# First MLP in four token groups of 432, attention values kept unsplit, last score rows on array quadrants

## The chip, the cores and the metric

One core of a Trainium2 chip runs one program. The metric is device time in microseconds (us); less is better. TensorE (PE) multiplies, with its weight loads shown as a stream of its own (PEld); VectorE (DVE), ScalarE (ACT) and GpSimd (POOL) do elementwise work; SyncE (SP) issues all DMAs from one queue, in order.

## The reference

Three stages in float32, 2304 tokens of 512 features:

```
scores = q @ k.T / 8, blocks of 64, block-causal mask   (batch 4, heads 8, seq 576, head_dim 64)
x = softmax(scores) @ v          -> tokens x 512
h = max(x @ w1, x @ w2, x @ w3)  -> 768 features;  y = h @ w_out          (first MLP)
u = max(y @ w_in, 0);  out = (u * u) @ w_out2     -> 2048 features, back to 512   (second MLP)
```

The four batch entries are independent in the attention only; in the MLPs every token is treated alike, so a group of tokens may be cut anywhere, across entries too.

## The kernel before

**Arithmetic.** TensorE has a fast format, float32r, that keeps fewer bits. For full precision most products are made of three float32r products: each operand is split into a high part (a cast) and a low part (the difference), and lo·hi, hi·lo and hi·hi are summed in PSUM. Where an operand is left as plain float32 (F32 tiles), one matmul in the program does the product, and the trace then shows two matmul records for it.

**Attention.** A pair of heads is one unit; 16 pairs, 4 for each entry. A pair has score steps of 128 rows (`step`, i = 0 to 3) and a last step (`last_step`) for its last 64 rows. Steps 0 and 1 belong to token group 0 (256 tokens), the others to group 1 (320 tokens). In the last step the 64 rows of both heads make 128 rows against 576 keys, in two halves of 288 keys (`sc_t0`, `sc_t1`), each in its own PSUM bank. For the four pairs of the first entry (`S_F32`) these scores are plain float32: one matmul for each head with a stationary tile of 128 rows and 64 columns, so two heads fill the two column halves of the array. For the other 12 pairs `score_operands` loads zero-padded queries `zt` and keys `kt`, splits both (`z2h`, `z2l`, `k2h`, `k2l`), and each half is three float32r matmuls of 128x128 by 288. Then come a maximum (DVE), an exponential (ACT), transposes against the identity (`tp`, PE) and the product with v (`av`, PE, column halves again).

**First MLP.** `mlp1(b, g)` handles one group: 18 accumulators of 12 matmuls (L1), then 4 accumulators of 18 (L2): 288 matmuls, each as wide as the group, 256 or 320 columns. There are 8 groups. Its input parts sit in `xhl0` and `xhl1`, one buffer for each group size, its hidden parts in `hh` and `hl`, one buffer each. The first entry's values are split as they leave PSUM; the other entries' values wait as float32 in `xf` and `split_x` splits them. The results `y` go to DRAM.

**Weight forms and second MLP.** All weights are converted on DVE, ACT and POOL. The second MLP's weights are turned into seven linear forms for each of 8 slices q (`up_forms`, `quad_forms`), split, and stored to DRAM; the second MLP (three passes of `up` and `down`, all matmuls 384 columns wide) streams them back through a ring of 9 tiles `ws`.

**Order.** All operations are recorded first, and a planner (`Plan.issue`) orders them by dependencies, ranks and the durations that `duration` gives. Attention has rank 0 and the first MLP rank 1, so MLP matmuls fill the gaps of attention. Every engine then runs its list strictly in order. The line of every operation in the profile is the planner's own, so the profile is read by tile names.

Of the kernel before, what the change touches and what calls it, by code (L numbers as in the profile page):

```python
# [12 lines left out]
F32 = mybir.dt.float32  # L13
# [11 lines left out]
NPAIR = H // 2  # L25
# [15 lines left out]
GA, GB = 256, 320  # L41
SCALE = 0.125
PAIRS = B * NPAIR

CFG = dict(PD=-1, PE=1, A1=0, A2=0, WP=1, FC=(8, 16), WO=24, FI=0, LO2=0, HI2=0, Q2=0, RN=3, XL=2, HL=2, SO=0, TF=0, W_A=0.7, W_B=1.5, SPARE='hl..rhl..rhl..r..r..r', S=15, PB=3, QB=(2, 2, 3), BANKS=(3, 2, 1, 2), LO=0, HI=0, Q=0, EV=('*', '*'), EV2=('a', 'a'), CB=2, PC=0, PM=1000, PX=-0.5, PO=0, HH='*', XH='*', N0='a', YS='a', HIS=0, RB=1, TB=(2, 1), KB=1, CT='a', LT='d', XA=4, XB=0)
# [302 lines left out]
def fused_kernel(ctx: ExitStack, tc: tile.TileContext, z0, k0, qk, v, w123, wo1, win2, wo2, out):  # L348
# [31 lines left out]
    def load_w_(src, hi, lo, name, f=None, raw=None):  # L380
        spare = SPARE[len(chunks)] if len(chunks) < len(SPARE) else "."
        chunks.append(name)
        if raw is not None:
            pass
        elif spare in "hl":
            both = m1.tile([128, 512, 3], U32, tag="h" + spare, name=f"raw_{name}").rearrange("p n t -> p (n t)")
            raw, f = both[:, :1024].rearrange("p (n t) -> p n t", t=2), both[:, 1024:].bitcast(F32)
        elif spare == "r":
            raw = at.tile([128, 512, 2], U32, tag="raw", bufs=CFG["RB"], name=f"raw_{name}")
            f = m1.tile([128, 512], F32, tag="xf", bufs=4, name=f"f_{name}")  # L390
# [68 lines left out]
    def score_operands(n):  # L459
# [27 lines left out]
        z2 = [z.rearrange("p h q -> p (h q)") for z in z2]  # L487
        return score, [(z2[1], k2[0]), (z2[0], k2[1]), (z2[0], k2[0])]
# [26 lines left out]
    def new_x(b, g):  # L515
        if (b, g) not in x_t:
            w = GROUPS[g][1]
            both = m1.tile([128, 2, KC, w], F32R, tag=f"xhl{g}", name=f"xhl{b}_{g}")
            x_t[b, g] = [both[:, i] for i in range(2)]
        return x_t[b, g]  # L520
# [8 lines left out]
    def attn_pair(n, groups=(0, 1)):  # L529
# [13 lines left out]
        if n not in xf_t and not direct:  # L543
            xf_t[n] = m1.tile([128, S], F32, tag="xf", bufs=4, name=f"xf{n}")
        xf = xf_t.get(n)
# [60 lines left out]
        def last_step():  # L606
# [31 lines left out]
        def values(g):  # L638
# [10 lines left out]
            if direct:  # L649
                rs = at.tile([128, GB], F32, tag="rs", name=f"rs{n}_{g}")  # L650
                nc.scalar.copy(out=rs[:, :w], in_=sum_rows(g)[:, :w])
                xh, xl = [t[:, n % NPAIR] for t in new_x(n // NPAIR, g)]
# [30 lines left out]
    def split_x(b, g):  # L683
        with nc.ranked(CFG["PX"]):
            split_x_(b, g)

    def split_x_(b, g):
        a, w = GROUPS[g]
        for hp in range(NPAIR):
            n = b * NPAIR + hp  # L690
            xf = xf_t[n][:, a:a + w]
            xh, xl = [t[:, hp] for t in new_x(b, g)]
            cp(CFG["XH"], out=xh, in_=xf)
            (nc.vector if CFG["XL"] == 2 or CFG["XL"] and b + 1 == B else nc.gpsimd).tensor_tensor(out=xl, in0=xf, in1=xh.bitcast(F32), op=ALU.subtract)
# [7 lines left out]
    def mlp1(b, g):  # L702
        with nc.ranked(1):
            mlp1_(b, g)

    def mlp1_(b, g):
        xh, xl = x_t[b, g]
        a, w = GROUPS[g]
        hh = m1.tile([128, NC1, GB], F32R, tag="hh", name=f"hh{b}_{g}")
        hl = m1.tile([128, NC1, GB], F32R, tag="hl", name=f"hl{b}_{g}")  # L710
# [7 lines left out]
        for c in range(NC1):  # L718
            run = None
            hi, lo = w1[c]  # L720
            for i in range(3):
                acc = acc_bank(f"l1_{b}_{g}_{c}_{i}")
# [4 lines left out]
                nxt = m1.tile([128, GB], F32, tag="run", bufs=CFG["RN"], name=f"run{b}_{g}_{c}_{i}")  # L727
# [6 lines left out]
            with urgent():  # L734
                cp(CFG["HH"], out=hh[:, c, :w], in_=run[:, :w])
                (nc.vector if CFG["HL"] == 2 or CFG["HL"] and b + 1 == B else nc.gpsimd).tensor_tensor(out=hl[:, c, :w], in0=run[:, :w], in1=hh[:, c, :w].bitcast(F32), op=ALU.subtract)
        for m in range(KC):
            acc = acc_bank(f"l2_{b}_{g}_{m}")
# [5 lines left out]
            ys = m1.tile([128, GB], F32, tag="ys", bufs=2, name=f"ys{b}_{g}_{m}")  # L744
            with urgent():
                cp(CFG["YS"], out=ys[:, :w], in_=acc[:, :w])
            nc.sync.dma_start(out=y_d[:, m, S * b + a:S * b + a + w], in_=ys[:, :w])
# [22 lines left out]
    mlp1(0, 0)  # L770
    for b in range(1, B):
        for _ in attention(b):
            pass
        if b == 1:
            if CFG["SO"]:
                split_x(1, 0)
            mlp1(0, 1)
        else:
            mlp1(b - 1, 0)
            if b + 1 < B:  # L780
                mlp1(b - 1, 1)
        if b + 1 < B:
            split_x(b, 0)
            split_x(b, 1)
# [12 lines left out]
    def quad_forms(s, q):  # L797
# [6 lines left out]
        s1 = at.tile([128, 256], F32, tag="ws1", name=f"ws1_{s}_{q}")  # L804
# [38 lines left out]
    RING = 9  # L843
# [8 lines left out]
    def up_forms(q):  # L852
        fa, fs = [w2p.tile([128, 4, 256], F32, tag="gq", bufs=5, name=f"w{x}{q}") for x in ("fa", "fs")]
# [14 lines left out]
    split_x(B - 1, 0)  # L868
# [68 lines left out]
    C_HOMES = [("xhl1", 3), ("hh", 2), ("hl", 2), ("wo1", 8), ("xhl0", 1)]  # L937
    g_c = {}

    def make_homes():  # L940
        places = []
# [9 lines left out]
    def split_g(p, name, j, f):  # L951
        home = turn_g[0] % 6
        turn_g[0] += 1
        both = (w2p.tile([128, 2, 2, TH], F32R, tag="gq", bufs=5, name=f"g{p}_{name}_{j}") if home else
                w1p.tile([128, 2, 2, TH], F32R, tag="w1l5", name=f"g{p}_{name}_{j}"))
        nc.scalar.copy(out=both[:, 0], in_=f)
        nc.vector.tensor_tensor(out=both[:, 1], in0=f, in1=both[:, 0].bitcast(F32), op=ALU.subtract)
        return both[:, 0], both[:, 1]

    def temp(tag, bufs, name):  # L960
        return m1.tile([128, TH], F32, tag=tag, bufs=bufs, name=name)
# [7 lines left out]
    def up(p, j):  # L969
# [53 lines left out]
    def down(p):  # L1023
# [5 lines left out]
        for name in DOWN:  # L1029
# [100 lines left out]
```

## Time and profile before

| what | value |
|---|---|
| runs (median of 3) | 856.17 us (855.03 to 856.58) |
| the profiled execution | 853.49 us, its span 851.7 us |
| granted TensorE clock, mean | 0.995 |
| PE busy | 834.9 us, 98% of the span |
| DVE, ACT, POOL busy | 638.5, 487.7, 130.0 us |
| DMA queue time, share of 16 engines | 67.4% |

The time of the profiled execution is its span and 1.8 us around it; it is 2.7 us below the median of the runs. The attention lies in the first 371 us, first-MLP work fills its gaps and goes on to 498 us, and the second MLP takes the rest. Start-to-start distances of matmuls are read from the timeline; a matmul's shown duration includes its passage through the array and overlaps the next one.

### The profile page before, as it was taken

To read this page: it belongs to the slowest core of one execution; us is meant where nothing else is said; L and a number is where in the kernel's file an instruction comes from. 1 tells how busy PE (TensorE), PEld (TensorE's weight loads), DVE (VectorE), ACT (ScalarE), POOL (GpSimd) and SP (SyncE) were. 2 spreads that over 40 slices of the span, in tenths; PEclk is the share of its full clock that TensorE was granted. 3 is DMA by queue.
4 is the path that set the end of the run, shared out by engine and by line. 5 is a ranking of instruction groups with operands and counts; after the bars stand their busy time and mean duration, and the time that the engine had idled before them with its cause. 6 is when DMAs were issued, how large, how long until landed. Compare 5 with 4: busy or idle time off the path is not lost.

```text
span 851.7 us, 16025 instructions
## 1 busy us (share of the span) xinstructions
PE 834.9 (98%) x5608; PEld 786.9 (92%) x5608; DVE 638.5 (75%) x1387; ACT 487.7 (57%) x1146; POOL 130.0 (15%) x126
## 2 busy tenths in 40 slices
PE   5999899999999999999999999999999999999998
PEld 3667799899999989999999999999999999999998
DVE  6997788888889888856676767788367867377662
ACT  7888778776787877755555422544232553133441
POOL 2233202122022021134535300000000000000000
PEclk9999999999999999999999999999999999999999
DMA  9745345465556446355777689898988888888882
GB/s 313 236 143 169 135 150 170 152 215 175 175 194 198 122 153 200 115 200 198 252 279 272 243 302 319 262 311 266 294 276 250 254 258 286 290 253 253 258 264 85
DMA packets 96623, 190.32 MB, mean 223 GB/s; under 512 B 13088, under 2 KB 23328, under 8 KB 96544
## 3 DMA queue, kind: packets, MB, share of 16 engines
q1 hardware_dynamic: 96544, 189.31, 67.4%
q8 instruction: 45, 0.74, 0.4%
q14 instruction: 34, 0.28, 0.1%
HBM read 150.47 MB, written 38.80 MB: 222 GB/s over the span
## 4 chain that ended last, share of the span: by engine, by line
PE 95%; DVE 1%; ACT 1%; DMA 1%; issue 0%; SPq 0%; POOL 0%; POOLq 0%; ACTq 0%
PE l L187 36%; PE acc_x L187 12%; PE ph_x L187 12%; PE ph_z L187 9%; PE acc_z L187 6%; PE av L187 6%; PE sc L187 6%; PE tp L187 4%; PE acc_y L187 3%; PE sc_t L187 2%; DMA zk<-in_k 1%; PE tp_t L187 1%; PE r L187 1%; ACT P L187 0%; SPq L187 0%
## 5 line engine op out<-in xcount | busy, mean ns | idle before, releaser
L187 PE MATMUL l<-xhl,w1h 128*128 128x320 f32 (+1 forms) x1152 | 244.5, 299 | 0.0
L187 PEld LDWEIGHTS l<-xhl,w1h 128*128 128x128 f32 x1152 | 188.0, 189 | 4.5 <-issue 2.9
L187 PE MATMUL l<-xhl,w1l 128*128 128x256 f32 (+1 forms) x576 | 174.5, 303 | 0.0
L187 PEld LDWEIGHTS l<-xhl,w1l 128*128 128x128 f32 x576 | 109.0, 189 | 3.4 <-issue 1.5
L187 PE MATMUL acc_x<-g_p,ws 128*128 128x384 f32 x576 | 102.2, 334 | 0.0
L187 PEld LDWEIGHTS acc_x<-g_p,ws 128*128 128x128 f32 x576 | 100.1, 188 | 0.0
L187 PE MATMUL l<-hh,wo 128*128 128x320 f32 (+1 forms) x384 | 82.7, 301 | 2.2 <-DVE wo L187 2.1
L187 PE MATMUL ph_x<-t,ws 128*128 128x384 f32 x432 | 80.7, 335 | 0.0
L187 PEld LDWEIGHTS ph_x<-t,ws 128*128 128x128 f32 x432 | 75.4, 188 | 0.0
L187 ACT ACTIVATE P<-sc,nm 128x128 f32<-128x128 f32 (+3 forms) x128 | 66.8, 531 | 8.7 <-DVE nm L187 6.3
L187 POOL TENSOR_TENSOR f_w<-f_w,raw_w 128x512 int32<-128x512 int32 x30 | 40.6, 1353 | 184.6 <-DVE f_w L187 44.9
L187 PEld LDWEIGHTS l<-hh,wo 128*128 128x128 f32 x384 | 64.2, 192 | 3.0 <-DVE wo L187 2.5
L187 DVE TENSOR_TENSOR run<-l,run 128x256 f32<-128x256 f32 (+1 forms) x96 | 43.7, 455 | 30.1 <-PE l L187 27.7
L187 PE MATMUL l<-hl,wo 128*128 128x256 f32 (+1 forms) x192 | 57.6, 301 | 0.0
L187 ACT CAST g_p<-c_wo 128x768 fp32r<-128x768 f32 x42 | 35.1, 836 | 38.4 <-PE acc_x L187 15.5
L187 DVE TENSOR_TENSOR g_p<-c_wo,g_p 128x768 fp32r<-128x768 f32 x42 | 39.9, 955 | 22.0 <-ACT g_p L187 21.8
L187 DVE TENSOR_REDUCE nm<-sc 128x2 f32<-128x256 f32 (+2 forms) x96 | 54.5, 588 | 0.6
L187 PE MATMUL ph_z<-b,ws 128*128 128x384 f32 x288 | 53.8, 335 | 0.0
L187 PE MATMUL tp<-ident,P 128*128 128x128 f32 x320 | 51.2, 275 | 1.4 <-ACT P L187 1.1
L187 PE MATMUL acc_z<-g_p,ws 128*128 128x384 f32 x288 | 51.2, 334 | 0.0
L187 PEld LDWEIGHTS ph_z<-b,ws 128*128 128x128 f32 x288 | 50.3, 188 | 0.0
L187 PEld LDWEIGHTS acc_z<-g_p,ws 128*128 128x128 f32 x288 | 50.1, 188 | 0.0
(170 smaller groups left out, 1640.1 us busy)
## 6 DMA issues: line engine op xcount, KB each, us to landing
ws<-ws_d SPq DMA_DIRECT2D x336, 256.0 KB, 3.9
ws_d<-wst SPq DMA_DIRECT2D x70, 256.0 KB, 3.4
raw<-in_qk SPq DMA_DIRECT2D x24, 576.0 KB, 3.8
ws_d<-wst SPq DMA_DIRECT2D x21, 512.0 KB, 6.4
raw_w<-in_w SPq DMA_DIRECT2D x18, 512.0 KB, 4.6
raw_w<-in_wo SPq DMA_DIRECT2D x16, 512.0 KB, 3.7
raw_wi<-in_win SPq DMA_DIRECT2D x14, 512.0 KB, 5.6
v<-in_v SPq DMA_DIRECT2D x16, 320.0 KB, 3.8
```

Of the source, the lines that this page charges most:

```text
L187: return getattr(engine, op_name)(*map(value, args), **{k: value(x) for k, x in kw.items()})
```

## The change

Five things change together.

1. The first MLP runs over 6 groups with edges 0, 256, 576, 1008, 1440, 1872, 2304: the last three entries become four groups of 432 tokens, two of which take tokens of two entries. `xhl` is one tile for the group at hand, so the split for the next group follows the last L1 matmul of this one. `hh`, `hl` grow to 432 columns.
2. The first entry's values of group 1 are kept unsplit in `xf` (now one tile for an entry, two of them) and split later by `split_x(0, 1)`.
3. The last score rows of the 12 later pairs are no longer split. One load, `kq` (one buffer, from a new input `ends`), holds for each head the 64 queries and 288 keys of half x in rows 64x to 64x+63. Each half and head is one float32 matmul on a stationary tile of 64 rows and 64 columns: four for a pair, one for each quadrant of the array. The planner's `duration` gives such a matmul a quarter of a full one's time.
4. The second MLP's sums `s1` to `s4` in `up_forms` move from POOL to DVE, and its tiles `gq` go from 5 buffers to 3.
5. Homes of tiles in the second MLP move to suit, and `ta` has one buffer in place of two.

The core of the diff:

```
-            return (4 * n / 2.4 + 5) * (0.5 if m == 64 else 1)
+            return (4 * n / 2.4 + 5) * (0.5 if m == 64 else 1) * (0.5 if m == 64 and n == HALF and stat.area.shape[0] == 64 else 1)
...
-        kt = at.tile([128, S], F32, tag="kraw", bufs=1 + CFG["TF"], name=f"kt{n}")
-        zt = at.tile([128, 2, 64], F32, tag="zraw", bufs=1 + CFG["TF"], name=f"zt{n}")
-        nc.sync.dma_start(out=kt, in_=k0[n])
-        nc.sync.dma_start(out=zt, in_=z0[n, :, :, TAIL:])
...
-        for f, (hi, lo) in ((kt, k2), (zt, z2)):
-            cp(CFG["CT"], out=hi, in_=f)
-            (nc.gpsimd if CFG["LT"] == "p" else nc.vector).tensor_tensor(out=lo, in0=f, in1=hi.bitcast(F32), op=ALU.subtract)
...
-        return score, [(z2[1], k2[0]), (z2[0], k2[1]), (z2[0], k2[0])]
+        kq = at.tile([128, 2, 64 + HALF], F32, tag="kq", bufs=1, name=f"kq{n}")
+        nc.sync.dma_start(out=kq, in_=ends[n - NPAIR])
+        return score, kq
...
-                    for c, (qp, kp) in enumerate(last):
-                        mm(sc[x][:, :HALF], qp, kp[:, ks], start=c == 0, stop=c == len(last) - 1)
+                    rows = slice(64 * x, 64 * x + 64)
+                    for h in range(2):
+                        mm(sc[x][64 * h:64 * h + 64, :HALF], last[rows, h, :64], last[rows, h, 64:], start=True,
+                           stop=True)
+            for x in range(2):
                 nc.vector.tensor_reduce(out=nm[:, x:x + 1], in_=sc[x][:, :HALF], axis=AX.X, op=ALU.max, negate=True)
...
-                xh, xl = [t[:, n % NPAIR] for t in new_x(n // NPAIR, g)]
+                if g:
+                    nc.vector.tensor_tensor(out=new_xf(n)[:, a:a + w], in0=acc[:, :w], in1=rs[:, :w], op=ALU.mult)
+                    return
+                xh, xl = [t[:, n % NPAIR] for t in new_x(g)]
...
-    def mlp1_(b, g):
-        xh, xl = x_t[b, g]
-        a, w = GROUPS[g]
+    def mlp1_(j):
+        xh, xl = x_t[j]
+        a, e = BLOCKS[j]
+        w = e - a
...
+    mlp1(0)
+    split_x(0, 1)
+    for _ in attention(1):
+        pass
+    mlp1(1)
+    split_x(1, 2)
+    for _ in attention(2):
+        pass
+    mlp1(2)
+    split_x(1, 3)
+    split_x(2, 3)
...
-            nc.gpsimd.tensor_tensor(out=o, in0=x, in1=y, op=op)
+            nc.vector.tensor_tensor(out=o, in0=x, in1=y, op=op)
```

What the planner makes of it is seen in the order of the built programs. The first place is PE at the first half of the last score rows of pair 8 (`sc8_t0`), between first-MLP matmuls `l1_...`, before:

```order
L187 MATMUL l1_1_0_2_0_2830<-xhl1_0_1539,w1l2_525 128x256
L187 MATMUL sc8_t0_2852<-k2h_8_2521,z2l_8_2574 128x288
L187 MATMUL sc8_t0_2852<-k2l_8_2561,z2h_8_2531 128x288
L187 MATMUL sc8_t0_2852<-k2h_8_2521,z2h_8_2531 128x288
L187 MATMUL l1_1_0_2_0_2830<-xhl1_0_1539,w1h2_508 128x256 x2
```

And now, with both halves of the same pair (`sc8_t0`, `sc8_t1`) and what stands next to them:

```order
L190 MATMUL tp8_1_0_2687<-ident_60,P8_1_0_2613 128x128 x2
L190 MATMUL sc8_t0_2697<-kq8_2479 64x288 x2
L190 MATMUL l1_2_0_2_2702<-xhl2_2303,w1l0_200 128x432
...
L190 MATMUL tp8_2_1_2738<-ident_60,P8_2_1_2676 128x128 x3
L190 MATMUL sc8_t1_2747<-kq8_2479 64x288 x2
L190 MATMUL l1_2_0_2_2702<-xhl2_2303,w1l0_200 128x432
```

The two heads of a half stand together, the two halves do not: eleven rows, with 128-row matmuls in them, lie between. In none of the 12 pairs does half 0 stand next to half 1. In 19 of the 24 halves the two heads stand together as here.

The second place is PE at `sc10_t0`, one of the five halves (`sc4_t0`, `sc9_t1`, `sc10_t0`, `sc13_t0`, `sc13_t1`) whose two heads stand apart now:

```order
L190 MATMUL l1_2_4_0_3253<-xhl2_2303,w1h4_748 128x432
L190 MATMUL sc10_t0_3276<-kq10_3047 64x288
L190 MATMUL tp10_1_0_3269<-ident_60,P10_1_0_3217 128x128 x2
L190 MATMUL sc10_t0_3276<-kq10_3047 64x288
L190 MATMUL l1_2_4_0_3253<-xhl2_2303,w1h4_748 128x432
```

Here transposes of 128 rows stand between the two heads.

The third place is SP's queue at the loads of pair 11 (`raw11_0`, `raw11_1` the two heads' queries and keys, `v11` its values), before:

```order
L187 DMA raw11_0_3444<-in_qk 128x1152
L187 DMA kt11_3460<-in_k0 128x576
L187 DMA zt11_3466<-in_z0 128x2x64
...
L187 DMA v11_0_3523<-in_v 128x640
L187 DMA y_d_1363<-ys1_0_3_3572 128x256
L187 DMA raw11_1_3642<-in_qk 128x1152
```

And now:

```order
L190 DMA raw11_0_3160<-in_qk 128x1152
L190 DMA ws_d1_3_3172<-wst1_3_1_3142 128x512
L190 DMA raw_w1_12_3206<-in_wo2 128x1024
L190 DMA v11_0_3209<-in_v 128x640
L190 DMA kq11_3336<-in_ends 128x704
L190 DMA raw11_1_3343<-in_qk 128x1152
```

`kq11` takes the one buffer that pair 10's last score matmuls read, and `raw11_1` now stands right behind it; so it is for pairs 5, 7, 11, 12 and 13.

## Rows read from the trace of the kernel before

**Rows 1.** Page: busy time of PE; the chain that ended last, by engine.
```profile
PE 834.9 (98%) x5608; PEld 786.9 (92%) x5608; DVE 638.5 (75%) x1387; ACT 487.7 (57%) x1146; POOL 130.0 (15%) x126
PE 95%; DVE 1%; ACT 1%; DMA 1%; issue 0%; SPq 0%; POOL 0%; POOLq 0%; ACTq 0%
```

**Rows 2.** Waits of PE: total us, times, longest.
```profile
PE sc L187 <- DMA zk<-in_k: 7.6, 3, 3.7
PE l L187 <- DVE wo L187: 2.1, 2, 1.7
```

**Rows 3.** L1 of one group of 320 and one of 256: ns, first to last start.
```profile
L187 PE MATMUL l<-xhl,w1h x144: 309/309/309, 379.4 to 410.8; 128*128 128x320 f32 x144
L187 PE MATMUL l<-xhl,w1l x72: 309/309/312, 379.3 to 410.5; 128*128 128x320 f32 x72
...
L187 PE MATMUL l<-xhl,w1h x144: 283/283/283, 421.6 to 447.3; 128*128 128x256 f32 x144
L187 PE MATMUL l<-xhl,w1l x72: 281/283/283, 421.5 to 447.1; 128*128 128x256 f32 x72
```

**Rows 4.** Windows: busy us (count) of PE, PEld, DVE, ACT, POOL; clock; DMA.
```profile
400.00:450.00 50.00, 50.00 (x386) 50.00 (x385) 35.14 (x64) 27.03 (x58) 25.11 (x24) 1.00 0.70 244
500.00:550.00 50.00, 50.00 (x291) 50.00 (x290) 35.15 (x60) 17.95 (x36) 0.00 (x0) 1.00 0.91 313
```

**Rows 5.** PE timeline, a float32r half: start, duration, operation, tiles, count.
```profile
114.90 0.60 PE L187 MATMUL tp<-ident,P 128*128 128x128 f32 x4
115.25 0.38 PE L187 MATMUL sc_t<-k2h,z2l 128*128 128x288 f32 x1
...
115.74 0.31 PE L187 MATMUL l<-xhl,w1h 128*128 128x320 f32 x1
```

**Rows 6.** Tile `sc_t` on PE, 105 to 375 us: one of three equal groups.
```profile
L187 PE MATMUL sc_t<-k2h,z2l x24: 288/298/406, 115.3 to 359.7; 128*128 128x288 f32 x24
```

**Rows 7.** PE timeline, a float32 half of a first-entry pair, heads together.
```profile
84.28 0.49 PE L187 MATMUL tp<-ident,P 128*128 128x128 f32 x3
84.70 0.46 PE L187 MATMUL sc_t<-k,z_qs 128*64 128x288 f32 x1
84.71 0.46 PE L187 MATMUL sc_t<-k,z_kl 128*64 128x288 f32 x1
...
85.34 0.39 PE L187 MATMUL l<-xhl,w1h 128*128 128x256 f32 x1
85.56 0.28 PE L187 MATMUL l<-xhl,w1l 128*128 128x256 f32 x1
```

**Rows 8.** PE timeline, a float32 half whose heads stand apart.
```profile
47.78 0.70 PE L187 MATMUL sc_t<-k,z_qs 128*64 128x288 f32 x2
48.41 0.55 PE L187 MATMUL tp<-ident,P 128*128 128x128 f32 x3
48.89 0.70 PE L187 MATMUL sc_t<-k,z_kl 128*64 128x288 f32 x2
49.52 0.50 PE L187 MATMUL l<-xhl,w1h 128*128 128x256 f32 x2
```

**Rows 9.** PE timeline, from first-MLP matmuls to column halves, and 64-row tiles.
```profile
116.61 0.45 PE L187 MATMUL l<-xhl,w1h 128*128 128x320 f32 x2
116.99 0.44 PE L187 MATMUL av<-ta,v 128*64 128x256 f32 x2
...
129.34 0.33 PE L187 MATMUL av<-t,v 64*64 64x64 f32 x4
129.60 0.42 PE L187 MATMUL l<-xhl,w1h 128*128 128x320 f32 x1
```

**Rows 10.** Groups by shape: splits of the last scores' operands; sums on POOL.
```profile
L187 ACT CAST k2h<-kt 128x576 fp32r<-128x576 f32 x12 | 8.2, 681 | 2.8 <-PE sc_t L187 2.7
L187 ACT CAST kh<-raw 128x576 fp32r<-128x576 f32 x24 | 16.2, 676 | 4.6 <-PE sc L187 4.6
L187 POOL TENSOR_TENSOR wfs<-wfa 128x256 f32<-128x256 f32 x14 | 12.7, 904 | 0.2
```

**Rows 11.** DMA issues: count, KB each, median us to landing.
```profile
raw<-in_qk SPq DMA_DIRECT2D x24, 576.0 KB, 3.8
ws_d<-wst SPq DMA_DIRECT2D x21, 512.0 KB, 6.4
```

More of the change, by code (lines that the diff above doesn't have):

```diff
@@ L347, in fused_kernel @@
 @with_exitstack
-def fused_kernel(ctx: ExitStack, tc: tile.TileContext, z0, k0, qk, v, w123, wo1, win2, wo2, out):
+def fused_kernel(ctx: ExitStack, tc: tile.TileContext, z0, k0, ends, qk, v, w123, wo1, win2, wo2, out):
     nc = Plan(tc)
@@ L513, in fused_kernel, with new_xf, new_x @@
     marks = []
[L515 to L520, printed above, removed]
+    def new_xf(n):
+        b, hp = divmod(n, NPAIR)
+        if b not in xf_t:
+            xf_t[b] = m1.tile([128, NPAIR, S], F32, tag="xf", bufs=2, name=f"xf{b}")
+        return xf_t[b][:, hp]
+    def new_x(j):
+        if j not in x_t:
+            a, e = BLOCKS[j]
+            both = m1.tile([128, 2, KC, e - a], F32R, tag="xhl", name=f"xhl{j}")
+            x_t[j] = [both[:, i] for i in range(2)]
+        return x_t[j]
     def prefetch(n, g):
@@ L542, in attn_pair @@
             t4 = at.tile([64, 2, 64], F32, tag="t4", bufs=2, name=f"t4_{n}")
-        if n not in xf_t and not direct:
-            xf_t[n] = m1.tile([128, S], F32, tag="xf", bufs=4, name=f"xf{n}")
-        xf = xf_t.get(n)
+        xf = None if direct else new_xf(n)
         def sc_tag(i):
@@ L681, in attn_pair, with split_x, split_x_ @@
             values(1)
[L683 removed]
+    def split_x(b, j):
         with nc.ranked(CFG["PX"]):
[L685 to L688 removed]
+            split_x_(b, j)
+    def split_x_(b, j):
+        a, e = [x - S * b for x in BLOCKS[j]]
+        src = slice(max(a, 0), min(e, S))
+        dst = slice(src.start - a, src.stop - a)
         for hp in range(NPAIR):
[L690 to L692 removed]
+            xf = xf_t[b][:, hp, src]
+            xh, xl = [t[:, hp, dst] for t in new_x(j)]
             cp(CFG["XH"], out=xh, in_=xf)
[L694 removed]
+            nc.vector.tensor_tensor(out=xl, in0=xf, in1=xh.bitcast(F32), op=ALU.subtract)
     @contextmanager
@@ L726, in mlp1_ @@
                            stop=k == KC - 1 and p == 2)
-                nxt = m1.tile([128, GB], F32, tag="run", bufs=CFG["RN"], name=f"run{b}_{g}_{c}_{i}")
+                nxt = m1.tile([128, 512], F32, tag="run", bufs=CFG["RN"], name=f"run{j}_{c}_{i}")
                 with urgent():
@@ L769, in fused_kernel @@
         f()
[L770 to L784, printed above, removed]
+    mlp1(0)
[9 more added lines that the diff above has]
+    split_x(2, 3)
+    for _ in attention(3):
+        pass
+    mlp1(3)
+    split_x(2, 4)
+    split_x(3, 4)
     def split_form(pool, tag, bufs, f, dest, name):
@@ L803, in quad_forms @@
         a11, a12, a21, a22 = quads if s == 0 else (quads[i] for i in (0, 2, 1, 3))
-        s1 = at.tile([128, 256], F32, tag="ws1", name=f"ws1_{s}_{q}")
+        s1 = at.tile([128, 256], F32, tag="rows", name=f"ws1_{s}_{q}")
         def split(x, form):
@@ L852, in up_forms @@
     def up_forms(q):
-        fa, fs = [w2p.tile([128, 4, 256], F32, tag="gq", bufs=5, name=f"w{x}{q}") for x in ("fa", "fs")]
+        fa, fs = [w2p.tile([128, 4, 256], F32, tag="gq", bufs=GQ, name=f"w{x}{q}") for x in ("fa", "fs")]
         if q == EARLY:
@@ L935, in next_unit @@
         return units[used[0] - 1]
-    C_HOMES = [("xhl1", 3), ("hh", 2), ("hl", 2), ("wo1", 8), ("xhl0", 1)]
+    C_HOMES = [("hh", 3), ("hl", 3), ("wo1", 8)]
     g_c = {}
+    g_home, keeps = [], {}
     def make_homes():
-        places = []
+        xhl = m1.tile([128, 2, 2, 2, TH], F32R, tag="xhl", name="g_xhl")
+        xf = [m1.tile([128, n, 2, TH], t, tag="xf", bufs=2, name=f"g_xf{n}") for n, t in ((3, F32), (2, F32R))]
+        g_home.extend((xhl[:, 0], xf[1], xhl[:, 1]))
+        for a in range(2):
+            keeps["p6", a] = m1.tile([128, TH], F32, tag="run", bufs=CFG["RN"], name=f"keep_p6_{a}")
+            keeps["p5", a] = xf[0][:, 2, a]
+        places = [xf[0][:, i] for i in range(2)]
         for tag, n in C_HOMES:
@@ L951, in split_g, with temp @@
     def split_g(p, name, j, f):
-        home = turn_g[0] % 6
+        home = turn_g[0] % 7
         turn_g[0] += 1
[L954 to L961, printed above, removed]
+        if home % 2:
+            hi, lo = [g_home[home // 2][:, i] for i in range(2)]
+        else:
+            both = (w2p.tile([128, 2, 2, TH], F32R, tag="gq", bufs=GQ, name=f"g{p}_{name}_{j}") if home else
+                    w1p.tile([128, 2, 2, TH], F32R, tag="w1l5", name=f"g{p}_{name}_{j}"))
+            hi, lo = both[:, 0], both[:, 1]
+        nc.scalar.copy(out=hi, in_=f)
+        nc.vector.tensor_tensor(out=lo, in0=f, in1=hi.bitcast(F32), op=ALU.subtract)
+        return hi, lo
+    def temp(name, a, p):
+        if name != "p1":
+            return keeps[name, a]
+        return m1.tile([128, TH], F32, tag="wf", bufs=2, name=f"{name}_{p}_{a}")
     BANKS_UP = ((("mlp", "mlp"), ("tp", "tp")), (("sc", "sc"), ("sc", "av")))
```

62 lines of the change are left out of this document (30 added, 32 removed).

## The prediction

> **What bounds the kernel now.** I read the page's busy times first, then the chain that ended last, then the waits of PE, then its timeline. PE is busy for 98% of the span and makes up 95% of the chain [rows 1]. Its waits are few and early: the first loads and one wait for converted weights, 2.1 us in all, are the largest two [rows 2]. From 400 us on every window of 50 us has PE busy for all 50 us [rows 4]. So the time is the sum of PE's start-to-start distances, and a change is worth what it does to that sum; work taken from DVE, ACT or POOL gives nothing by itself unless PE waits for it.
>
> **First MLP in wider groups.** The last three entries now take 3 x 576 matmuls (three of 288 at 256 columns, three of 288 at 320), 1728 in all; after the change 4 x 288 = 1152 of 432 columns, for the same number of columns in total. What falls away is the fixed part of 576 matmuls. The 216 matmuls of one L1 start between 379.3 and 410.8 us at 320 columns, so one takes 31.5/215 = 0.1465 us; at 256 columns 25.8/215 = 0.1200 [rows 3]. A column costs (0.1465 - 0.1200)/64 = 0.000414 us, so 432 columns should take 0.1465 + 112 x 0.000414 = 0.193 us. The second MLP's 384 columns fit: 50 us for some 290 matmuls is 0.173 [rows 4]; 48 columns more would make 0.193 too. Before: 3 x 288 x (0.1200 + 0.1465) = 230.3 us. After: 1152 x 0.193 = 222.3 us. Gain about 7.8 us (7.5 to 8.0 by the rounding of the starts). It is all on the path, since PE has no idle time to lose it in.
>
> **Last score rows on quadrants.** A float32r half costs little now. In [rows 5] the three matmuls take 115.25 to 115.74 = 0.49 us, but the four transposes ahead of them start only 0.35 us earlier, where each costs 0.11 (a run of four shows 0.60 us, one of three 0.49 [rows 5, 7]), so 0.09 us comes back: 0.40 us net. There are 24 such halves [rows 6]: 9.6 us.
>
> The new halves are float32 on 64-column tiles. The nearest rows are the first entry's halves, with 128 rows instead of 64. With the heads together [rows 7], the transposes ahead take 0.42 us for three in place of 0.33 (0.09 on the way in), the half takes 84.70 to 85.34 = 0.64 us with the two heads starting 0.01 us apart, and the next MLP matmul takes 85.34 to 85.56 = 0.22 us where 0.12 is usual (0.10 on the way out): 0.83 us for a visit. From MLP matmuls the way in costs the same: the two at 116.61 take 0.38 us to the `av` at 116.99 in place of 0.29 [rows 9]. With the heads apart [rows 8], each head is a visit of its own: 0.09 + 0.63, then 0.48 us for three transposes in place of 0.33 (0.15), then 0.63 + 0.10: 1.60 us for the half.
>
> In the order now, 19 halves have their heads together and 5 have them apart, and no half 0 stands next to its half 1. So the four quadrants never run together; only two columns' worth do, as in the first entry. The sum is 19 x 0.83 + 5 x 1.60 = 23.8 us, against 9.6: a loss of 14.2 us. The planner could put them apart without seeing a price, since its durations hold no switch. That a 64-row tile runs as long as a 128-row one is not shown at this size. Below, a visit could cost its bare passes: 0.11 us for 128 columns of a transpose makes 0.25 for 288, two passes 0.49, and 29 visits 14.2 us, a loss of 4.6. Above, another 0.09 for the change of the tile's height makes 29 x 0.09 = 2.6 more, a loss of 16.8. That two 64-row tiles with different columns run side by side is seen where four records of `av` take 0.26 us in all [rows 9], so twice the time is excluded. I take 14.2, by the nearest rows.
>
> The Trainium skill bears on this (TensorEngine Tiling (Array Packing), Key Properties): changing the tiling mode, not just the tile, drains TensorE. The trace agrees, with the 0.09 us in and 0.10 us out above. The same section says that different tiles load and multiply in parallel; that would need the four matmuls of a pair side by side, and is weighed as a rival.
>
> **What leaves ACT, DVE and POOL.** 12 pairs lose the casts and differences of keys and queries, 0.68 us each for the cast of the keys alone [rows 10]; 12 us on ACT and about as much on DVE. PE did not wait for them after 105 us, so I count nothing. The one place is the wait for `wo` [rows 2]: the first entry's group-1 values and pair 4's operands leave ACT and DVE just ahead of it, some 2 to 4 us of work on two engines that are not wholly full. Bounds: all 2.1 us gone, or as much again added, as `ta` has one buffer; I take a gain of 0.3.
>
> **What comes to DVE and to the buffers.** 28 sums of 256 columns move from POOL, where they take 0.9 us [rows 10], to DVE, which is busy for 35 of 50 us there [rows 4]. Were they as slow on DVE, 25 us over some 120 us would bring it to 45 or 46 of 50. The form chain has 3 buffers for 5, but the order still has the last forms in the last L1, with all of L2 (72 x 0.193 = 14 us) ahead of the second MLP. Nothing, with a price of a few us if that chain slips. The single `xhl` puts the split (8 to 16 casts and differences of half a microsecond) between one group's L1 and the next; L2 of 10 to 14 us and attention cover it. The second MLP's homes change no PE work. Nothing for either; up to 2 us above.
>
> **Sum.** -7.8 + 14.2 - 0.3 = +6.1 us. The profiled execution of 853.5 us would become 859.6. The runs' median lies 2.7 us above it, so I put the time at 862.
>
> **Rivals.** *A visit costs only its bare passes.* If the smaller tile needs no drain, 29 x 0.49 us is 4.6 us over the old cost, the MLP's gain wins, and the sum is 4.6 - 7.8 - 0.3 = -3.5: about 852.5. It decides below (9.6 + 7.8 + 0.3)/29 = 0.61 us a visit. For it: no row has this tile at this size. Against: the 0.09 and 0.10 us are seen on every visit of the column halves, and leaving 64-row tiles [rows 9] the next matmul at 129.60 still shows 0.42 us of duration where its kind has 0.31 [rows 3].
>
> *Four at once.* If the two halves of a pair somehow overlapped, a pair would cost one visit: 12 x 0.83 = 10.0 us, a loss of 0.4, and the sum is -7.7: about 848. Against it is the order, with 128-row matmuls between the halves, and PE starts its matmuls in order throughout the timeline. The Trainium skill's rule that tiles work in parallel (TensorEngine Tiling (Array Packing), Key Properties) would give this only for neighbours, which they are not.
>
> *SP's queue.* The load of `kq` waits for PE's last scores of the pair before, and for five pairs the next pair's second raw load stands right behind it. From there 3.8 us to landing [rows 11], two ACT passes of 0.7 [rows 10] and PE's first use must follow; between them PE has work for some 8 us (at pair 11, 32 MLP matmuls at 0.193 and small ones). With a landing like the slow stores' 6.4 us [rows 11] and a busy ACT, 1 us is missed at each, 5 us in all: 867. It decides if landing and casts pass 8 us. The planner saw this wait, and PE is slower than it planned, which gives slack.
>
> *Nearly no change*, a visit of about 0.62 to 0.70 us and the rest as forecast: 854.5 to 858.
>
> **Chances.** Forecast 0.70 (859 to 865, its own range); bare passes 0.08; four at once 0.03; SP's queue 0.10; nearly no change 0.09. About 0.2% (1.7 us) can be told from no change. Faster 0.11, same 0.09, slower 0.80. The range 855.5 to 868 leaves out the two fast rivals, and a few in a hundred above.
>
> **What would show it.** In the profile after: L1 of a 432 group with 216 starts in 41.5 us; 29 visits of `sc_t<-kq`, each 0.6 us and more from its first start to the next matmul, heads within 0.01 us of each other, a slow neighbour on either side; PE busy for whole windows after 105 us; and the second MLP starting some 6 us later than 498. If a visit is 0.5 us with normal neighbours, the score term is wrong. If new waits of PE on ACT, DVE or DMA appear after 105 us, the cover was less than I say.

## The result and the profile after

| kernel | runs | median | range |
|---|---|---|---|
| before | 4 | 855.6 us | 853.7 to 856.6 |
| after | 4 | 868.09 us | 867.3 to 869.0 |

The ratio is 1.0149 (95% interval 1.0127 to 1.0172): slower by 12.5 us where 6.1 was forecast. The profiled execution of after took 868.98 us with a span of 867.2. Its page, and the waits of PE, answer to [rows 1, 2]:

```profile
PE 847.8 (98%) x5056; PEld 769.1 (89%) x5056; DVE 630.5 (73%) x1350; ACT 476.6 (55%) x1095; POOL 107.4 (12%) x98
PE 94%; ACT 2%; DVE 1%; DMA 1%; issue 0%; SPq 0%; POOL 0%; ACTq 0%; POOLq 0%; DVEq 0%
```

```profile
PE sc L190 <- DMA zk<-in_k: 6.2, 3, 3.5
PE tp L190 <- ACT P L190: 4.5, 4, 2.8
PE l L190 <- DVE wo L190: 2.7, 1, 2.7
```

PE is still the bound: 552 fewer matmul records, 12.9 us more of busy time. The wait for `wo` has not gone but grown to 2.7 us. The waits for `P` have grown too, from 1.1 to 4.5 us, but they lie ahead of 40 us, where PE is idle for 11.5 us in after and for 10.9 and 10.6 in two profiles of before: they mostly stand in for other waits. To see where the time came from, look at the first start of the second MLP (tile `ph_x`; ns min/median/max, then first and last start). After:

```profile
L190 PE MATMUL ph_x<-b,ws x144: 331/335/339, 513.4 to 792.6; 128*128 128x384 f32 x144
```

Before, profiled a second time (run f1_before_again below):

```profile
L187 PE MATMUL ph_x<-b,ws x144: 331/335/336, 498.7 to 777.4; 128*128 128x384 f32 x144
```

Of the 15.1 us between the spans of these two executions 14.7 are there ahead of the second MLP. Next, PE's timeline of after around one visit to the small tiles (start, duration, operation, tiles, count), the answer to [rows 5, 7], and the group of all such matmuls:

```profile
208.36 0.38 PE L190 MATMUL tp<-ident,P 128*128 128x128 f32 x2
208.68 0.70 PE L190 MATMUL sc_t<-kq 64*64 64x288 f32 x4
209.31 0.46 PE L190 MATMUL l<-xhl,w1l 128*128 128x432 f32 x1
209.61 0.55 PE L190 MATMUL l<-xhl,w1h 128*128 128x432 f32 x2
```

```profile
L190 PE MATMUL sc_t<-kq x96: 402/428/454, 118.7 to 375.2; 64*64 64x288 f32 x96
```

Two transposes take 0.32 us where 0.22 is usual, the two heads 0.63, the next matmul 0.30 where 0.195 is its kind's: 0.83 us, as forecast. The 96 records are two for each float32 matmul of 12 pairs, two halves and two heads, and they come in 29 visits.

L1 of one of the new groups, the answer to [rows 3]:

```profile
L190 PE MATMUL l<-xhl,w1h x144: 353/357/365, 457.3 to 499.0; 128*128 128x432 f32 x144
L190 PE MATMUL l<-xhl,w1l x72: 353/358/362, 457.1 to 498.6; 128*128 128x432 f32 x72
```

216 starts in 41.9 us, 0.195 us apart where 0.193 was expected. Last, the windows around the wait for `wo` (busy us of PE, PEld, DVE, ACT, POOL; granted clock; DMA). After, then before in its second profile, then two of the windows in before's first profile:

```profile
104.00:108.00 4.00, 1.37 (x12) 1.16 (x10) 2.18 (x6) 1.08 (x2) 1.41 (x1) 1.00 0.54 169
108.00:112.00 4.00, 3.59 (x14) 3.10 (x15) 2.17 (x7) 1.79 (x4) 0.00 (x0) 0.53 0.18 15
112.00:116.00 4.00, 4.00 (x23) 4.00 (x23) 1.77 (x6) 1.98 (x9) 0.00 (x0) 0.62 0.61 198
90.00:120.00 30.00, 26.45 (x180) 22.31 (x179) 22.87 (x56) 20.04 (x52) 5.82 (x4) 0.89 0.32 102
```

```profile
104.00:108.00 4.00, 2.18 (x16) 1.77 (x16) 1.94 (x3) 2.55 (x6) 0.98 (x1) 1.00 0.34 136
108.00:112.00 4.00, 4.00 (x37) 4.00 (x36) 2.81 (x9) 1.93 (x9) 0.00 (x0) 1.00 0.63 193
90.00:120.00 30.00, 27.82 (x221) 24.65 (x220) 23.16 (x60) 22.47 (x59) 5.74 (x4) 1.00 0.34 111
```

```profile
104.00:108.00 4.00, 3.44 (x19) 3.24 (x20) 1.91 (x3) 1.99 (x4) 0.00 (x0) 0.74 0.20 66
108.00:112.00 4.00, 4.00 (x30) 4.00 (x30) 2.47 (x9) 1.99 (x9) 0.00 (x0) 0.83 0.58 180
```

After loses 1.4 us more to idling between 90 and 120 us, and after the idle time TensorE's granted clock is at its lower level (0.53 and 0.62 over two windows of 4 us, 1.2 GHz for most of them); PE then does 14 matmuls where before's second profile has 37. Before's first profile has the lower level here too, for a shorter time (0.74 and 0.83), so the low clock as such did not come with the change.

### The profile page after: what moved, and what is told of

Read it like the earlier page. It is cut to its first block, busy times and chain, and to the rows that moved or that the text cites. A ratio compares the mean times of both kernels' runs of the same rounds, so it can differ in the third digit from the quotient of the medians.

```text
span 867.2 us, 14714 instructions
## 1 busy us (share of the span) xinstructions
PE 847.8 (98%) x5056; PEld 769.1 (89%) x5056; DVE 630.5 (73%) x1350; ACT 476.6 (55%) x1095; POOL 107.4 (12%) x98
## 4 chain that ended last, share of the span: by engine, by line
PE 94%; ACT 2%; DVE 1%; DMA 1%; issue 0%; SPq 0%; POOL 0%; ACTq 0%; POOLq 0%; DVEq 0%
PE l L190 35%; PE ph_x L190 12%; PE acc_x L190 12%; PE ph_z L190 9%; PE acc_z L190 6%; PE av L190 6%; PE sc L190 5%; PE tp L190 4%; PE acc_y L190 3%; PE sc_t L190 2%; PE tp_t L190 1%; DMA raw<-in_qk 1%; DMA zk<-in_k 1%; ACT P L190 0%; PE r L190 0%
## 5 line engine op out<-in xcount | busy, mean ns | idle before, releaser
L190 PE MATMUL l<-xhl,w1h 128*128 128x432 f32 (+2 forms) x864 | 230.8, 344 | 0.0
L190 PE MATMUL l<-xhl,w1l 128*128 128x432 f32 (+2 forms) x432 | 148.3, 345 | 0.7 <-ACT run L190 0.5
L190 PE MATMUL l<-hh,wo 128*128 128x432 f32 (+2 forms) x288 | 79.7, 349 | 2.7 <-DVE wo L190 2.7
L190 ACT ACTIVATE P<-sc,nm 128x128 f32<-128x128 f32 (+3 forms) x128 | 67.0, 532 | 12.9 <-DVE nm L190 10.3
L190 DVE TENSOR_TENSOR run<-l,run 128x432 f32<-128x432 f32 (+2 forms) x72 | 40.1, 556 | 30.3 <-PE l L190 27.9
L190 PEld LDWEIGHTS tp<-ident,P 128*128 128x128 f32 x320 | 39.4, 143 | 17.0 <-ACT P L190 6.9
L190 PE MATMUL acc_x<-g_p,ws 128*128 128x384 f32 x288 | 54.4, 335 | 0.0
L190 PE MATMUL l<-hl,wo 128*128 128x432 f32 (+2 forms) x144 | 50.6, 352 | 0.0
L190 PEld LDWEIGHTS acc_x<-g_p,ws 128*128 128x128 f32 x288 | 50.5, 188 | 0.0
L190 PE MATMUL av<-tb,v 128*64 128x320 f32 (+1 forms) x256 | 35.5, 412 | 0.4 <-ACT tb L190 0.4
L190 DVE TENSOR_SCALAR P<-P,sm 128x128 f32<-128x128 f32 (+3 forms) x96 | 35.2, 400 | 0.4
```

The lines of the kernel that those rows point to most:

```text
L190: return getattr(engine, op_name)(*map(value, args), **{k: value(x) for k, x in kw.items()})
```

## The experiments

Before ran beside each at a median of 855.2 to 855.4 us. Two theories stood at first. **A**: the small-tile visits cost what was forecast, and something else ate the gain. **B**: something else is the early phase, with the wait for `wo` and the low clock behind it.

**e1_quadrants_alone.** Before with the new last score rows and nothing else (`score_operands` and `last_step` as in the change).

> The kernel before with the quadrant scores alone (one unsplit load for a pair, float32 tiles of 64 rows and 64 columns; groups of 256 and 320, POOL and buffers as before). Theory A (each place where such tiles stand among 128-row matmuls costs 0.83 us, read from the trace after: 0.09 in, 0.63, 0.10 out): 22 halves together and 2 with heads apart make 22 x 0.83 + 2 x 1.60 = 21.5 us against 9.6, so about +12 us on the kernel before, near 867.5. Theory B (the loss came mostly from the early wait for the first MLP's last weights and from the wide groups): at most +4, near 858 or below.

867.15 us (865.6 to 869.9), ratio 1.0152 (1.012 to 1.0184): +11.8 by the medians. Its trace has 26 visits: 22 halves with the heads together and two apart, by the forecast's prices 22 x 0.83 + 2 x 1.60 - 9.6 = +11.9. The score rows alone cost as much as the whole change.

**e2_four_together.** After, with the four small matmuls of a pair forced next to each other (what is recorded in `glued()`, new too, the planner issues as one piece):

```
...
+            if not sf:
+                with nc.glued():
+                    for x in range(2):
+                        rows = slice(64 * x, 64 * x + 64)
+                        for h in range(2):
+                            mm(sc[x][64 * h:64 * h + 64, :HALF], last[rows, h, :64], last[rows, h, 64:], start=True,
+                               stop=True)
...
```

> The changed kernel with the four quadrant matmuls of a pair forced to stand next to each other on PE. Theory A with four at once: 12 visits of 0.83 in place of 23.8 us, so -13.8 us on the changed kernel, near 854. Theory A with only two columns at a time: 12 visits of 0.19 + 2 x 0.64 = 1.47, so -6 us, near 862. Theory B: within 3 us of the changed kernel.

853.41 us (852.3 to 855.4), ratio 0.9981 (0.9967 to 0.9994): 14.7 us below after, and below before. PE's timeline of this kernel:

```profile
206.41 0.47 PE L190 MATMUL l<-xhl,w1l 128*128 128x432 f32 x1
206.80 0.72 PE L190 MATMUL sc_t<-kq 64*64 64x288 f32 x8
207.45 0.87 PE L190 MATMUL tp<-ident,P 128*128 128x128 f32 x6
```

All four matmuls (eight records) now take 0.65 us, as two did in after. A pair costs one visit in place of two or more.

**e3_full_tile_float32.** The same precision without small tiles: one float32 matmul of 128x128 for a half, with zero-padded queries.

```
...
+        return score, [(zt.rearrange("p h q -> p (h q)"), kt)]
...
+                    for c, (qp, kp) in enumerate(last):
+                        mm(sc[x][:, :HALF], qp, kp[:, ks], start=c == 0, stop=c == len(last) - 1)
...
```

> The changed kernel with the last scores of the 12 pairs as one unsplit float32 matmul of 128 rows and 128 columns for each half (zero-padded queries, no operand split, no tiles smaller than the array). Theory A (the price is the switch to small tiles and back): a half costs its two passes, 0.49 us, wherever it stands: 24 x 0.49 = 11.8 in place of 23.8, so -12 us, near 856. Theory C (unsplit float32 is itself the price): no gain, within 3 us of 868. Theory B: the same, within 3 us.

858.03 us (856.2 to 859.0), ratio 1.0041 (1.0021 to 1.006). 10 us below after at the same precision, without leaving the 128x128 tile. PE's timeline around one such half:

```profile
206.37 0.38 PE L190 MATMUL tp<-ident,P 128*128 128x128 f32 x2
206.59 0.65 PE L190 MATMUL sc_t<-kt,zt 128*128 128x288 f32 x2
206.86 0.77 PE L190 MATMUL l<-xhl,w1h 128*128 128x432 f32 x2
207.47 0.36 PE L190 MATMUL l<-xhl,w1l 128*128 128x432 f32 x1
```

The two transposes take their usual 0.22 us. From the half's first start to the third `l` 0.88 us go by, of which two `l` take 0.39: the half costs 0.49 us, as expected, where a visit to the small tiles costs 0.83. So float32 is not the price; the small tile is, with 0.20 us on the way in and out and 0.14 because the same 288 columns take 0.63 us there.

**e4_first_split_later.** After, with `split_x(0, 1)` given rank 0.5 in place of -0.5, behind attention, so that its casts and differences don't stand ahead of the last `wo` by rank.

> The changed kernel with the split of the first entry's second group ranked behind the weight conversions instead of ahead of them. Theory B1 (this split ran on ACT and DVE just ahead of the last weights and made PE wait 2.7 us, whereupon its clock fell for 6.8 us): the wait goes back to 1 us or less and 3 to 5 us come off, near 864. Theory B2 (the last weight's own chain of load, ACT, DVE and POOL is late, whatever is split): within 1.5 us of the changed kernel.

867.95 us, ratio 1.0156 (1.0135 to 1.0177), the wait for `wo` 2.5 us and the clock low as in after. But the edit did not clear the way: DVE's timeline of e4 has three of the four differences right ahead of the last `wo` all the same.

```profile
103.81 2.20 DVE L190 TENSOR_TENSOR xhl<-xf,xhl 128x320 fp32r<-128x320 f32 x3
105.94 0.68 DVE L190 TENSOR_TENSOR wo<-f_wo,wo 128x512 fp32r<-128x512 f32 x1
```

So the run says nothing against theory B1; it left the mechanism open.

**f1_before_again.** The kernel before, unchanged, profiled once more.

> The kernel before, unchanged, profiled once more, to see how much of its early phase repeats. Theory L (the old profile was lucky early): its first low spell of TensorE's clock ends later than at 6.95 us, or the first MLP's last converted weight comes later than 103.7 us, and the second MLP starts at 500 to 501 us instead of 498.3. Theory S (the early phase of before repeats): 498.3 us within 0.5, and the whole early excess of 5 us belongs to the change.

853.94 us; second MLP at 498.7 us, wait for `wo` 2.1 us in all. The early phase of before repeats in its length, though not in its clock (the windows of both profiles are shown above).

**f2_four_together_narrow.** e2 with groups of 256 and 320 again:

```
-EDGES = (0, GA, S, *(1008, 1440, 1872, 2304))
+EDGES = tuple(S * b + x for b in range(B) for x in (0, GA)) + (T,)
...
```

The tiles stay 432 columns wide, and the calls of `mlp1` and `split_x` follow the groups.

> The kernel of the run e2_four_together (853.41 us), with the last three entries in six groups of 256 and 320 tokens again instead of four of 432, nothing else changed. Theory by the measured pitch (432 columns take 0.1956 us): 1728 matmuls take 230.3 us, 1152 take 225.3, so the narrow groups cost 5.0 us: 858.4. Theory by the prediction (0.193 us): 222.3 against 230.3, 861. Theory N (the wide groups gain nothing because the time comes back elsewhere): 853.4 to 854.5.

859.40 us (858.1 to 860.3), ratio 1.0049 (1.0031 to 1.0068): the wide groups are worth 6.0 us, some 2 either way by the intervals. That excludes theory N; the 0.195 of the row above gives 230.3 - 1152 x 0.195 = 5.7. The forecast's 7.8 lies within the 2 us of this run, so it is the row that decides against it. Of the 6.0 us the profiles put 1.0 in the second MLP: from its first `ph_x<-b` to its last it takes 280.0 us here and 279.0 in e2.

**f3a_weights_at_0_8 and f3c_weights_slope_2.** e2 with other paces for recording the weight conversions (`W_A=0.8, W_B=1.7` and `W_A=0.7, W_B=2.0`).

> The kernel of the run e2_four_together with two of the planner's constants for the pace of the first MLP's weight conversions changed (W_A 0.7 to 0.8, W_B 1.5 to 1.7), so that the last weight's steps stand earlier in DVE's list. Theory B2 (the wait for the last weight and the low clock behind it are the lost early time): the wait of 2.7 us shrinks below 1 us, the low spell of 6.8 us falls to 3.4 us or none, and the time is 849 to 851.5. Rival (the early phase is short of work whatever the order): the time stays at 852.5 to 854.5, the idle time goes elsewhere ahead of 115 us.

> The same as the run f3a_weights_at_0_8 with the constants 0.7 and 2.0, which put the last weight's last step 5 places earlier in DVE's list than in e2_four_together. Theory B2: wait below 1 us, no low spell of 6.8 us, 849 to 851.5. Rival: 852.5 to 854.5 with the idle time elsewhere ahead of 115 us.

856.22 us (ratio 1.0009, 0.9994 to 1.0024) and 860.78 us (1.0065, 1.0045 to 1.0085): both slower than e2. In f3a the clock from 90 to 120 us is full and the time still goes, as that window and its waits at 202 us show:

```profile
90.00:120.00 30.00, 25.09 (x194) 20.55 (x192) 22.61 (x61) 22.01 (x57) 5.15 (x4) 1.00 0.36 120
```

```profile
202.22 0.67 PE L190 MATMUL l<-xhl,w1l 128*128 128x432 f32 x2 [0.69 <-ACT xhl L190]
203.26 0.46 PE L190 MATMUL l<-xhl,w1h 128*128 128x432 f32 x1 [0.37 <-DVE xhl L190]
```

4.9 us of idle time between 90 and 120 us, against 3.2 in e2, and new waits of 1.1 us later. The wait for `wo` itself did not shrink in f3a: it comes in three pieces, 3.8 us in all. In f3c it is gone and that clock is full, as theory B2 asked, and the time is 7.4 us longer than e2's; a new wait stands at 61 us,

```profile
60.80 1.04 PE L190 MATMUL tp<-ident,P 128*128 128x128 f32 x4 [3.42 <-ACT P L190]
```

with a mean clock of 0.66 from 60 to 65 us behind it, and waits of 1.6 and 1.0 us follow at 106 and 109 us. Mending one place is not mending the phase; theory B2 as put there fell.

**What is late on DVE.** The traces then gave a mechanism for e2 and after. DVE's timeline of after, ahead of the last `wo`:

```profile
82.73 1.57 DVE L190 TENSOR_SCALAR f_wo<-f_wo 128x512 int32<-128x512 int32 x1 [0.17 <-ACT f_wo L190]
...
95.67 0.42 DVE L190 TENSOR_SCALAR f_wo<-f_wo 128x512 int32<-128x512 int32 x1
96.53 1.85 DVE L190 TENSOR_TENSOR xhl<-xf,xhl 128x320 fp32r<-128x320 f32 x2
...
101.91 0.85 DVE L190 TENSOR_SCALAR f_wo<-f_wo 128x512 int32<-128x512 int32 x1 [0.38 <-ACT f_wo L190]
```

POOL's, of the same kernel:

```profile
82.71 1.30 POOL L190 TENSOR_TENSOR f_wo<-f_wo,raw_wo 128x512 int32<-128x512 int32 x1 [3.83 <-ACT f_wo L190]
96.32 1.31 POOL L190 TENSOR_TENSOR f_wo<-f_wo,raw_wo 128x512 int32<-128x512 int32 x1 [3.83 <-DVE f_wo L190]
100.68 1.80 POOL L190 TENSOR_TENSOR f_wo<-f_wo,raw_wo 128x512 int32<-128x512 int32 x1 [3.05 <-DVE sm L190]
```

A shift of 0.42 us that starts under POOL's addition ends 0.28 to 0.29 us after it: 1.57 and 0.85 us. So do the differences `xhl<-xf`, a second kind of work that the unsplit values bring: two take 1.85 us where 0.48 each is usual. In before the same difference reads the value from PSUM, and one that starts under an addition is not delayed; POOL and then DVE of before:

```profile
101.72 1.30 POOL L187 TENSOR_TENSOR f_wo<-f_wo,raw_wo 128x512 int32<-128x512 int32 x1 [3.60 <-DVE f_wo L187]
```

```profile
102.39 0.49 DVE L187 TENSOR_TENSOR xhl<-av,xhl 128x320 fp32r<-128x320 f32 x1 [0.43 <-ACT xhl L187]
```

The trace agrees with the Trainium skill (SBUF — State Buffer, Who interferes with whom): a DVE step with two SBUF inputs contends with a GpSimd step that reads SBUF, one in a mode that uses two ports contends with GpSimd too, and whichever issues second is blocked in full; with at most one SBUF input, outside those modes, a DVE step does not contend. Summed over all DVE steps ahead of 112 us that ran over 0.15 us longer than the median of their kind, each of them started under POOL work: 5.5 and 5.9 us in the two profiles of before, 3.4 in e1, 2.8 in h3 (below), 9.0 in after and in e2, 8.0 in f2. From 80 us on it is 0.5 in before, 1.0 in e1 and h3, 3.6 in after. Only 1.0 us of that lies on the differences; the rest lies on steps of a kind that before has too, which in the new order start under POOL's work.

**g2_weight_adds_on_DVE.** Meant to move POOL's additions for `wo` to DVE.

> The kernel of the run e2_four_together with the six integer additions of the wo conversion moved from POOL to DVE (DVE may lose the last bits of these weights; nothing else is left out). In the changed kernel's trace three DVE steps that start while POOL adds for wo end only with it (1.57 us and 0.85 us for shifts of 0.42, 1.45 us for a difference of 0.48): 2.5 us of DVE lost ahead of the last weight, against 0 in the kernel before. Theory S (these stalls make the last weight late): they vanish, six additions of about 0.7 us come to DVE and POOL's 1.3 us leave the chain; the last weight is ready 2 us or more earlier, the wait falls from 2.7 below 1.5 us, the low spell from 6.8 to 3.4 us, time 849.5 to 852. Rival (DVE's list is simply too long there): 4.1 us more of work, wait of 2.5 us or more, 853 to 856.

The edit's condition asked for tile names that begin with `wo_`, while they begin with `wo1_`, so nothing moved: the program of e2 ran a second time. 852.64 us (850.9 to 855.0), ratio 0.9969 (0.9954 to 0.9984). It is a repeat of e2, and says nothing on theory S. It shows what one program's early phase varies by: here the wait for `wo` is 3.0 us and the window from 90 to 120 us has a mean clock of 0.94, in e2's profile 2.7 and 0.89.

**g3_first_values_split_at_once.** e2 with the first entry's values split as they leave PSUM:

```
-                if g:
-                    nc.vector.tensor_tensor(out=new_xf(n)[:, a:a + w], in0=acc[:, :w], in1=rs[:, :w], op=ALU.mult)
-                    return
...
-    split_x(0, 1)
```

> The kernel of the run e2_four_together with the change's second part undone: the first entry's values of group 1 are split as they leave PSUM again (group 0's input parts stand in the free buffer of xf), all else as there. The difference then has one input in PSUM; from xf it has both in SBUF. Theory U (the unsplit values made the early loss): DVE's stalls ahead of 112 us fall from 9.0 us to 5 or 6, the wait for wo to 1.7 to 2.2 us, the low spell from 6.8 to 3.4 us, PE's excess between 90 and 120 us from 7.4 to about 4, and the time to 849 to 851.5. Rival (the planner's new order as a whole, not this part, lost the time): 852.5 to 854.5 with a wait of 2.5 us or more.

854.00 us (852.3 to 856.4), ratio 0.9982 (0.9969 to 0.9995): no change from e2. Yet the early part of theory U came true: DVE's delays fell from 9.0 to 3.8 us, the wait for `wo` from 2.7 (3.0 in g2) to 2.1, PE's idle time from 90 to 120 us from 3.2 (3.5) to 2.5. The clock of that window is 0.94 in place of 0.89, but g2, without this edit, has 0.94 too, so that can't be put down to it. DVE's differences of these values between 50 and 112 us, in g3:

```profile
L190 DVE TENSOR_TENSOR xhl<-av,xhl 128x320 fp32r<-128x320 f32 x4 | 1.9, 486 | 1.0 <-ACT xhl L190 1.0
```

A wait that e2 does not have stands at 198 us, at the first L1 of group 2, as PE's timeline of g3 shows:

```profile
198.02 0.28 PE L190 MATMUL sc<-kl,qs 128*128 128x256 f32 x1
199.01 0.66 PE L190 MATMUL l<-xhl,w1l 128*128 128x432 f32 x2 [0.71 <-ACT xhl L190]
200.21 0.46 PE L190 MATMUL l<-xhl,w1h 128*128 128x432 f32 x1 [0.54 <-DVE xhl L190]
```

A like wait stands in f3a (above). A group of 432 takes in values of rows that a group of 256 did not need; the reading that the next run tests is that PE has no other work there when pair 7's values are late.

**h2_group2_without_pair7.** g3 with that dependency taken away; the kernel leaves out pair 7's values in this group and takes pair 6's in their place:

```
-            xf = xf_t[b][:, hp, src]
+            xf = xf_t[b][:, 2 if (j, hp) == (2, 3) else hp, src]
```

> The kernel of the run g3_first_values_split_at_once (854.00 us; the early stalls of DVE are down from 9.0 to 3.8 us there, and yet the time is that of e2_four_together), in which the first 432-token group of entry 1 takes pair 6's values in place of pair 7's: pair 7's values are left out of that group, so its input no longer waits for them. PE's order is the same up to 177 us. Theory C (what is won early is given back at 198 us, where this group's first L1 matmuls wait 0.7 and 0.5 us for the split of pair 7's values, which come at 198 us in both kernels): those waits vanish, the second MLP starts at 496 to 497 us instead of 498.2, time 852 to 852.6. Rival (the time is lost elsewhere, the wait only marks it): 853.5 to 854.5.

853.28 us (849.8 to 854.9), ratio 0.9970 (0.9956 to 0.9985). The waits at 198 us are gone, as forecast, but the time is within the uncertainty of g3's. In the profile the second MLP starts at 499.7 us, but this execution was late before the waits: where the two kernels' order on PE first differs it stands at 183.6 us, g3's at 181.1, after a lower clock (0.89 from 90 to 120 us, in the same order as g3's 0.94). From there to the second MLP it takes 316.1 us, g3 317.1. It has a new wait further on, at 384 us:

```profile
PE av L190 <- ACT tb L190: 0.9, 1, 0.9
```

That pair 7's values set the wait at 198 us is shown; that the wait is all that kept the early gain from counting is not.

**h3_four_together_alone.** Before with only the four together (e1's edit with e2's).

> The kernel before with only its last score rows changed, on quadrants with the four matmuls of a pair side by side; groups, values, xhl, sums and homes as before. Theory A: a pair costs one visit of about 0.83 us, 12 x 0.83 = 10.0 against 9.6 us for the float32r halves, so 855.3 to 856.2 against 855.3, and the rest of the change is worth e2_four_together minus this, -2.5 us or so, not the -8.1 of the forecast. Rival (all but the scores gives what was forecast, and the four together still cost 5 us): 860 or more.

856.68 us (854.7 to 862.1), ratio 1.0015 (0.9999 to 1.0031): the rival (860 or more) falls. So all but the scores is worth e2 - h3 = -3.3 us (-4.0 by the repeat), not -8.1; with the narrow groups (f2 - h3) it is +2.7 us, with 2 either way.

## Why the prediction was wrong

The direction was right, and the size was half of what came; the measured 868.09 us lies just outside the range of 855.5 to 868. No one term made the miss: against the forecast the scores came out 1.8 us dearer, the width 1.8 to 2.1, and the rest 3.0, and of these the scores' 1.8 is within the uncertainty of 2.

**Score rows: right.** 0.09 in, 0.63, 0.10 out was measured as written, the two heads start 7 ns apart, and 29 visits came. By the runs the price is h3 - before (1.3 us by its ratio) + after - e2 (14.7) = 16.0 us against 14.2, with some 2 us either way. The rival "bare passes" is out, and so is "nearly no change"; its 0.49 us is what a half takes on the full tile (e3), not on the small one. (By the prediction's own terms "nearly no change" comes to 856.5 to 858.8 us, not 854.5 to 858; nothing hung on that.) The rival "four at once" was right in its mechanism and in its condition: e2 made the matmuls neighbours, and the loss went. Its 848 us was too low for the reason that the forecast was: the two terms below.

**The term of the 432-wide groups: mis-sized, -7.8 where -5.7 (rows) or -6.0 (f2) was measured.** The step that failed is "A column costs (0.1465 - 0.1200)/64 = 0.000414 us, so 432 columns should take 0.193 us". The second MLP's 384 columns fitted the line, but 432 lie beyond them, and there the pitch is 0.195; 1152 matmuls make some 2 us of that.

**The term of ACT, DVE and POOL: the step that failed.** "PE did not wait for them after 105 us, so I count nothing. [...] I take a gain of 0.3." No gain came. Work leaving DVE was counted; that the work staying there changes its kind and its place was not. The unsplit values turn the difference into one with two SBUF inputs, just ahead of the last `wo`, where POOL is adding, and in the new order other DVE steps fall under POOL's work as well. The wait for `wo` is 2.7 to 3.0 us in after, e2, g2 and f2, where before, e1 and h3 have 2.0 to 2.2, and PE's idle time from 90 to 120 us is 3.2 to 3.6 us against 2.2 to 2.6. g3 and h2, with the values split at once, are back at 2.1 and 2.5: for the delays, the wait and the idle time the cause is shown. For the time it is not, since g3's did not move. "As much again added" (2.1 us) stood as the upper bound.

In time, all but the scores and the width is worth +2.7 us (f2 - h3), with 2 either way, and not all of that is early: 1.4 us of it lies in the second MLP, which takes 280.0 us in f2 and 278.6 in h3 (first `ph_x<-b` to last). The other way, e2 - h3 (-3.3, -4.0 by the repeat) less the width's -5.7 and the 0.4 by which e2's second MLP is longer than h3's leaves 1.3 to 2.0 us for the early phase, no more than the uncertainty.

**What comes to DVE and the buffers: nothing, nearly right.** In after PE is never idle for 0.15 us or more at a time behind 112 us, and the second MLP takes 0.6 us longer (in f2 1.4 us longer than in h3; "up to 2 us above" was allowed for). In g3 PE did wait 1.3 us at 198 us, for the wider group's later values (h2); the like 1.1 us in f3a was not taken apart. SP's queue gave no wait.

**The sum.** By the runs: 16.0 (scores) - 6.0 (width) + 2.7 (the rest) = 12.7 us, against 14.2 - 7.8 - 0.3 = 6.1. (The differences between h3, f2, e2 and after add up to the whole by construction; directly measured it was 12.5.) What stays open is what the rest consists of in time. The delays on DVE are shown, but undoing them did not shorten the kernel. The low clock does not go by the wait ahead of it: the window from 90 to 120 us has 0.89 behind 2.7 us (e2) and behind 2.1 (h2), 0.94 behind 3.0 (g2) and behind 2.1 (g3). Over all runs the mean clock is 0.9950 in h3 and 0.9939 in f2, so an estimate from these is that it explains at most 0.0011 x 857 = 0.9 us of the 2.7. And why f2's second MLP is 1.4 us longer was not followed up.

Best of all runs is e2's program: 853.41 and 852.64 us, 0.2 to 0.3% below before.

## What to carry to other kernels

Price a visit to another tile shape as way in plus way out, about 0.2 us here, plus the passes as they run on that shape (0.63 us where the full tile takes 0.49), and then fill it: four quadrants side by side cost what two cost. Where a pitch is extended to a new width, take a row wider than the new one as well. And when a value's home moves from PSUM to SBUF, count each later DVE step on it as one that may have to wait for POOL, and look at what the new order puts under POOL's work besides and at what is queued behind it. Take a second profile before a stretch of low clock is put down to a change.

## What the runs showed of the hardware

- Four float32 matmuls on the four 64x64 quadrants of the array take 0.65 us together; two on one half of its rows take 0.63 (e2 and after). The Trainium skill (TensorEngine Tiling (Array Packing), Key Properties) says that tiles work independently; here that holds where nothing of another shape stands between them.
- A tile of 64 rows is not faster than one of 128 with the same 64 columns: 288 float32 columns take 0.63 us (after) and 0.64 ([rows 7]). On the full 128x128 tile they take 0.49 (e3).
- Matmuls of the first MLP start 0.120 us apart at 256 columns, 0.1465 at 320 ([rows 3]) and 0.195 at 432 (after), where the line through the first two gives 0.193.
- DVE's shift of 512 columns takes 0.42 us alone and 1.57 us when it starts under POOL's addition (after); a difference with one input in PSUM keeps its 0.49 us (before).
- How long TensorE's clock stays at its lower level behind a wait differs between executions of one program: behind the wait for `wo` the window from 90 to 120 us has a mean of 0.94 and 1.00 in the two profiles of before (waits of 1.7 us), 0.89 and 0.94 in those of e2's program (2.7 and 3.0 us).
